# Sums of the output-weight quarters: from GpSimd subtractions to ScalarE negations and adding transfers

## The chip, the core and the metric

The kernel runs on one core of a Trainium2 chip. The metric is the device time of one execution in microseconds (us); the time before is the median of three executions, 1373.9 us (1372.88 to 1374.18). The profile is of one further execution, whose span is 1369.5 us. The engines are called PE (TensorE), DVE (VectorE), ACT (ScalarE), POOL (GpSimd) and SP (SyncE, which only issues transfers here).

## What is computed

An attention block with a threshold, followed by a feed-forward block. Cut to what matters:

```python
# q, k, v: (8, 8, 576, 64) float32; tau: a scalar
scores = q @ k.T / sqrt(64)
thresh = max(scores, -1) - tau
scores = where(scores >= thresh, scores, -1e9)
attn = softmax(scores)                      # exp, divided by the sum + 1e-9
x = (attn @ v), heads side by side          # (4608, 512)
# w_in: (512, 2048), w_out: (2048, 512)
h = x @ w_in
g = h / (1 + exp(-1.702 * h))
out = g @ w_out                             # (4608, 512) float32
```

The feed-forward weights arrive as float64 and are converted to float32 on the chip.

## The kernel before

**Attention** goes by pairs of heads, 32 pairs `n` in all, four to a batch. For each pair PE makes transposed scores in five tiles (`scores`, `scores_two`, `tail_scores`, lines 462 to 487), ACT copies them out of PSUM (`keep`, `keep_two`, L498 and L512), DVE finds maxima (`in_groups` L526, then `over_tiles` L532 and L537, then `over_groups` L546 and L547, small operations on 64 or 32 partitions), DVE subtracts the threshold (`sub`, L598), ACT masks (L609) and exponentiates (L613), PE multiplies by the values (`values`, L627), and DVE sums, inverts and places the product into `xT` (L698). POOL copies a small key tail into `kd` for the fifth score tile (`prep_kd`, L452).

**Feed-forward** goes by blocks of 256 rows. The first two blocks are done plainly by `first_blocks`: `mm1_0` (L753), tanh, gelu, `mm2` (L735), and `half` (L742), an ACT copy with a scale out of PSUM. From block `PLAIN` = 2 on, `feed_forward` computes the hidden layer with `mm1` (L713), ACT's `tanh` (L722) and DVE's `gelu` (L725), which frees one of two PSUM banks for the next `mm1`. The second product (`second`, `product`, L900) is Strassen-Winograd's: both the gelu output and `w_out` are cut into four quarters, and seven products of quarters or sums of quarters replace eight. The last four blocks use the same scheme for the first product too (`two_blocks`, `product1`, L818).

The gelu output's sums are made for each block on POOL (`s_sums`, L866 to L868, and `s_last`, L879). The sums of the quarters of `w_out` are made once and stay. With `qb[f][m]` the quarters of `w_out` (each 128 partitions by 8 rows by 256 columns):

```python
t1, t2, t4 = tw
t3 = qb[0][1]
T_SUMS = [(t1, t3, qb[0][0]), (t2, qb[1][1], t1), (t4, qb[1][0], t2), (t3, qb[1][1], t3)]   # out = a - b
```

`t3` is made in place of a quarter of `w_out`, and `t4` lies where `first_blocks` keeps its gelu output; both may be written only when the first two blocks are done. `t1` and `t2` need only the converted `w_out`. In the kernel before, the four sums are eight POOL operations of half a quarter each, queued after the first `s_sums` of block 2. The products that read them are P6 (`t2`), P7 (`t3`), P4 (`t4`) and P5 (`t1`).

**The order of work.** All engines' instructions are put in order when the program is built, by a planner in the kernel: `task(engine, cost, rank, function, ..., after, take, give, lag)` names a cost in us, a rank, the tasks it waits for, the buffers it takes and gives, and the time from its end until others may use its result. `run_in_order` plays this forward: a free engine takes the ready task of lowest rank whose buffers are free. Feed-forward products on PE have rank `LAST`, so they fill what attention leaves; tanh, gelu and sums have `FIRST`. On the chip each engine works its list in that order and waits at each instruction for its semaphores. So a change of a task's engine, cost or lag moves other instructions too. Weight conversion is also among these tasks: `load_w` (POOL transfers, L399 and L400), `cv_power` on ACT (L418), and `cv_end` on DVE (L436), which writes a piece of `w_in` or `w_out`.

Of the kernel before, what the change touches and what calls it, by code (L numbers as in the profile page):

```python
# [14 lines left out]
AF = mybir.ActivationFunctionType  # L15
ALU = mybir.AluOpType
# [14 lines left out]
def kernel(  # L31
# [34 lines left out]
    nc = tc.nc  # L66
# [11 lines left out]
    HF = d_ff // P // 2  # L78
# [132 lines left out]
    def task(engine, cost, rank, f, *a, after=(), take=(), give=(), lag=None):  # L211
        if lag is None:
            lag = LAG[engine]
        if 0 <= rank < LAST:
            rank += CV.get(f.__name__, 0.0) + (EARLY if a[0] < 2 * NPAIR else LATER).get(f.__name__, 0.0)
        tasks.append((engine, cost, rank, f, a, [x for x in after if x is not None],
                      take, give, lag))
        return len(tasks) - 1

    FIRST, LAST = -9.0, 1000.0  # L220
# [101 lines left out]
    def own(n, *pools):  # L322
        return tuple(x + "_apart" for x in pools) if n in APART else pools
# [33 lines left out]
    n_in = len(pieces)  # L357
# [7 lines left out]
    def stage(i):  # L365

        if i < n_in:
            return i % (STAGES + 2) if i % (STAGES + 2) < STAGES else None
        i -= n_in
        return STAGES - 1 if i % 3 == 0 and i < NFC - PER_STAGE else None  # L370
# [376 lines left out]
    PLAIN = 2  # L747
# [107 lines left out]

    T_SUMS = [(t1, t3, qb[0][0]), (t2, qb[1][1], t1), (t4, qb[1][0], t2), (t3, qb[1][1], t3)]

    def t_sum(x, k):
        o, a, b = (y[:, ts(k, 4), :] for y in T_SUMS[x])
        nc.gpsimd.tensor_tensor(out=o, in0=a, in1=b, op=ALU.subtract)  # L860

    def s_sums(k):

# [18 lines left out]
    P1, P2, P6, P7, P4, P5, P3 = range(7)  # L882
# [56 lines left out]
    for h in range(2):  # L939
        nc.gpsimd.memset(ones_t[ts(h, D), h, :], 1.0)  # L940
    nc.gpsimd.dma_start(
        out=tau_b, in_=bass.AP(tensor=tau.tensor, offset=tau.offset, ap=[[0, P], [1, 1]])
# [28 lines left out]
    WHOLE = 6  # L971

    FFU = 1.727

    W_IN, W_OUT = (3.11, 1.53), (2.49, 2.62)
    ready_w, w_loads = [], []
    for i in range(len(pieces)):
# [7 lines left out]
        x = stage(i)  # L985
        place = ("w64",) if x is None else (f"stage{x}",)
        a = task("POOL", 1.1, rank, load_w, i, after=w_loads[-1:], take=place, lag=9.0)
# [3 lines left out]
        a = task("DVE", 1.1, rank, cv_frac, i, after=[e])  # L991
# [8 lines left out]
    placed, spread, ffn = {}, {}, []  # L1000
    last_mm2, t_ready = {}, []

    def first_blocks():
        xs = list(placed.values())[-NPAIR:]
        for j in range(NFC):
            for i in range(PLAIN):
                x = j * P // WC
                ffn.append(task(
                    "PE", FFU, LAST, mm1_0, j, i,
                    after=ffn[-1:] + xs + ready_w[x * NDC : (x + 1) * NDC],  # L1010
# [4 lines left out]
        for i in range(PLAIN * BLK // P):  # L1015
            for p in range(NFC // 2):
                after = ffn[-1:] + [gelus[2 * p], gelus[2 * p + 1]]
                after += ready_w[n_in + 2 * p : n_in + 2 * p + 2]
                ffn.append(task(
                    "PE", FFU, LAST, mm2, i, p, after=after, take=("psM",) if p == 0 else (),  # L1020
                ))
# [2 lines left out]
            task("SP", 0.6, FIRST, store_0, i, after=[a], give=("osb",), lag=2.2)  # L1024


    def feed_forward(blk):
        b = -(-(blk + 1) * BLK // S) - 1
        xs = [placed[n] for n in range(NPAIR * (b + 1))]
        sums = []  # L1030
        for j in range(HF):
            for f in range(2):
                after = ffn[-1:] + xs[-NPAIR:]
                last = j == HF - 1 and f == 1
                ffn.append(task(
                    "PE", FFU, LAST, mm1, blk, j, f, after=after,
                    take=("psM",) if f == 0 else (), give=("xT",) if last else (),
                ))
            a = task("ACT", 0.48, FIRST, tanh, j, after=ffn[-1:], take=("io",))
            gelus[j] = task(  # L1040
                "DVE", 0.59, FIRST, gelu, j, after=[a, last_mm2.get(j // 4)],
                give=("psM", "io"),
            )
            if j % 2:
                sums.append(task("POOL", 2.3, FIRST, s_sums, j // 2, after=[gelus[j - 1], gelus[j]]))
            if j == 1 and blk == PLAIN:
                for y in range(8):
                    after = t_ready[-1:] + sums[-1:] + ready_w[n_in:]
                    t_ready.append(task("POOL", 2.4, FIRST, t_sum, *divmod(y, 2), after=after))
        second(blk, 0, {j: [gelus[j]] for j in range(HF)}, sums)  # L1050

    T_OF = {P6: 4, P7: 8, P4: 6, P5: 2}

    def second(blk, w, ready, sums):
        reads = [None] * 7
# [3 lines left out]
        for x, p in order:  # L1059
            js = ((0, 4), (4, 8), (4, 7), (7, 8))[p]  # L1060
            after = ffn[-1:]
            if x in T_OF:
                after += t_ready[: T_OF[x]]
            if x in (P1, P2, P4):
# [3 lines left out]
            else:  # L1068
# [3 lines left out]
            ffn.append(task(  # L1072
                "PE", FFU / 4 * (js[1] - js[0]), LAST, product, blk, x, js, w, after=after,
                take=("psA" if w else "psM",) if x in (P1, P2) and p == 0 else (),
# [19 lines left out]
    def two_blocks(blk):  # L1094
# [18 lines left out]
        for j in range(HF):  # L1113
            reads = [None] * 7
            for x in range(7):
# [6 lines left out]
                if x == P3 or first:  # L1122
                    after += xs
                bank = (BANK_OF[(7 * j + x) % 5],)
                ffn.append(task(
                    "PE", FFU / 2, LAST, product1, blk, j, x, after=after, take=bank,
                    give=("xT", "xT") if x == P3 and j == HF - 1 else (),
# [33 lines left out]
    for n in range(NP):  # L1161
        gate = per_pair * (n - LEAD)
        after = ffn[gate : gate + 1] if gate >= 0 else []
# [7 lines left out]
        lag = (4.6, 3.0)[n] if n < 2 else 10.0 if n < 2 * NPAIR else 3.0  # L1171
# [18 lines left out]
        for t in range(NKT + 1):  # L1190
            tail = t == NKT
            copies = []
            if n >= WHOLE and not tail:
                if t % 2 == 0:
                    a = task(
                        "PE", 1.94, r, scores_two, n, t, after=[pq, pk] + after,
                        take=("psA",) * 3 + ("s_m",) * 2,
                    )
                    after = [a]
                b = task("ACT", 0.6, r, keep_two, n, t, 0, after=[a], give=("psA",))  # L1200
# [5 lines left out]
            elif tail:  # L1206
                a = task(
                    "PE", 0.97 * slow, r, tail_scores, n, after=[pq, pk, pd] + after,
                    take=("psA", "s_t"), give=own(n, "qkT0", "qkT1") + ("kd",),
                )  # L1210
                after = [a]
                copies = [task("ACT", 0.55, r, keep, n, t, 0, after=[a], give=("psA",))]
            else:
                for c in range(2):

                    a = task(
                        "PE", 0.49 * slow, r, scores, n, t, c, after=[pq, pk] + after,
                        take=("psA",) + (own(n, "s_m") if c == 0 else ()),
                    )
                    after = [a]  # L1220
                    copies.append(task("ACT", 0.55, r, keep, n, t, c, after=[a], give=("psA",)))
            mx.append(task("DVE", 0.66 if tail else 1.27, r, in_groups, n, t, ALU.max, after=copies))
        a = task("DVE", 0.8, r, over_tiles, n, ALU.max, after=mx)
        a = task("DVE", 0.86, r, over_groups, n, ALU.max, after=[a])
        if n in BY_DMA:
            a = task("DVE", 0.5, r, lower_rows, n, after=[a, tau_done], take=("row",))
            a = task("SP", 0.35, r, row_out, n, after=[a], lag=3.3)
            m = task(
                "SP", 1.5, r, row_in, n, after=[a], take=own(n, "mb") + ("mbt",), give=("row",),
                lag=5.2,  # L1230
            )
        else:
            a = task("DVE", 0.68, r, lower, n, after=[a, tau_done])
# [3 lines left out]
        for t in range(NKT + 1):  # L1237
            tail = t == NKT
            a = task(
                "DVE", (0.67 if n in BY_DMA else 1.55) if tail else 1.35, r, sub, n, t, after=subs[-1:],  # L1240
                give=own(n, "mb") + (("mbt",) if n in BY_DMA else ()) if tail else (),
            )
            subs.append(a)
            a = task("ACT", 0.59 if tail else 1.09, r, mask, n, t, after=[a])
# [3 lines left out]
        if n < NPAIR:  # L1248
# [12 lines left out]
            a = task("DVE", 1.07, r, one_row, n, after=[den], give=("psM", "psM"))  # L1261
        else:
            pv = task("PE", 4.84, r, values, n, every, after=ws + [lv], take=("psA",), give=("v_m", v_tail))
        if NPAIR <= n < BY_PE:
            a = task("PE", 4.84, r, sums_by_pe, n, every, False, after=ws + [pv], take=("psA",), give=back)
            a = task("DVE", 1.07, r, one_row, n, after=[a], give=("psA",))
        elif n >= BY_PE:
# [4 lines left out]
            a = task("DVE", 0.8, r, over_tiles, n, ALU.add, after=su + [pv], give=back)  # L1272
            a = task("DVE", 0.86, r, over_groups, n, ALU.add, after=[a])
            a = task("DVE", 0.75, r, one_group, n, after=[a])
        a = task("DVE", 1.05, r, spread_sums, n, after=[a], take=("rc",))
        b, hp = divmod(n, NPAIR)
# [6 lines left out]
        while hp == NPAIR - 1 and (next_blk + 1) * BLK <= (b + 1) * S:  # L1283
            if next_blk >= TAIL:
                if (next_blk - TAIL) % 2:
                    two_blocks(next_blk - 1)
            elif next_blk >= PLAIN:
                feed_forward(next_blk)
            elif next_blk == PLAIN - 1:
                first_blocks()  # L1290
            next_blk += 1
# [31 lines left out]
```

## Time and profile before

| | before |
|---|---|
| time, median of three | 1373.9 us |
| span of the profiled execution | 1369.5 us |
| `t_sum` on POOL (L860) | 8 operations of 128x1024 float32, 2343 to 2375 ns, from 290.7 to 309.2 us |
| ACT, all work | 638.0 us (47% of the span) |
| DMA | 78.70 MB in all, mean 57 GB/s |

How to read it: an engine's busy time counts instructions that run, also while they are held up inside. "Idle before" names the wait that ended last before an instruction. PE's busy time contains matmuls at whatever clock was granted, so PE can be busy and slow. The waits with the largest sums in the page are on engines with much idle time (POOL for gelu outputs, ACT for matmuls) and say nothing on the time by themselves.

### The profile page before, as it was taken

What the parts mean: (1) busy time and instruction counts of PE and PEld (TensorE: products, weight loads), DVE (VectorE), ACT (ScalarE), POOL (GpSimd) and SP (SyncE); (2) the same over time, 40 slices, a digit from 0 to 9 for tenths busy, and PEclk for the clock granted to TensorE, in tenths of its full rate; (3) what the DMA queues carried; (4) which work ended last, traced back from release to release, by engine and by line L of the source; (5) the groups of instructions that cost most, each with busy time, mean ns of one, the idle gap of its engine ahead of it and who ended that gap; (6) DMA issues with size and microseconds to landing.
All of it is one profiled execution on the core that took longest, in us unless ns stands there. A gap on an engine that the chain in (4) does not pass through costs nothing.

```text
span 1369.5 us, 18133 instructions
## 1 busy us (share of the span) xinstructions
PE 1315.9 (96%) x6792; PEld 1010.6 (74%) x6792; DVE 1111.1 (81%) x1906; ACT 638.0 (47%) x822; POOL 279.9 (20%) x362
## 2 busy tenths in 40 slices
PE   5769999988999999999999999999999999999999
PEld 3436764466777877787777777787778778888887
DVE  7899999899999889818999889929999698562642
ACT  4875565455455455415555455424655453110210
POOL 1202210053121211311120312021222204420120
PEclk9998999998999999999999999999999999999999
DMA  8775774111210111101112111201211000000000
GB/s 166 258 200 195 252 242 107 39 26 24 57 26 15 42 22 39 30 21 18 42 33 47 24 34 26 47 5 43 43 27 43 9 16 1 16 1 16 16 0 31
DMA packets 205379, 78.70 MB, mean 57 GB/s; under 512 B 192747, under 2 KB 192747, under 8 KB 205291
## 3 DMA queue, kind: packets, MB, share of 16 engines
q1 hardware_dynamic: 195723, 43.71, 15.0%
q0 software_dynamic: 7200, 33.55, 7.0%
q8 instruction: 53, 0.87, 0.3%
q10 hardware_dynamic: 2368, 0.30, 0.2%
q14 instruction: 35, 0.29, 0.1%
HBM read 68.05 MB, written 9.47 MB: 57 GB/s over the span
## 4 chain that ended last, share of the span: by engine, by line
PE 64%; DVE 23%; ACT 8%; issue 3%; DMA 1%; SPq 1%; DVEq 0%; ACTq 0%
PE ops L900 20%; PE hps L713 13%; PE pv L627 9%; PE ps L487 5%; DVE part L526 5%; PE ps L818 4%; DVE arena L598 4%; PE ps L900 4%; PE ops L735 3%; ACT arena L613 3%; ACT arena L609 3%; PE ops L818 3%; DVE arena L725 2%; PE ps L472 2%; DVE arena L572 1%
## 5 line engine op out<-in xcount | busy, mean ns | idle before, releaser
L713 PE MATMUL hps<-xT,w_in 128*128 128x256 f32 x1536 | 343.2, 382 | 10.9 <-DVE arena L725 10.9
L713 PEld LDWEIGHTS hps<-xT,w_in 128*128 128x128 f32 x1536 | 290.8, 191 | 61.4 <-DVE arena L725 14.3
L526 DVE TRANSPOSE_TENSOR_REDUCE part<-arena 128x36 f32<-128x1152 f32 x236 | 310.6, 1349 | 25.9 <-ACT arena L498 24.2
L900 PE MATMUL ops<-w_out,arena 128*128 128x256 f32 x896 | 206.4, 382 | 2.9 <-DVE arena L725 2.9
L613 ACT ACTIVATE arena<-arena,shift,scl 128x1152 f32<-128x1152 f32 (+1 forms) x160 | 200.0, 1250 | 4.5
L900 PEld LDWEIGHTS ops<-w_out,arena 128*128 128x128 f32 x896 | 168.1, 190 | 36.5 <-issue 8.3
L609 ACT ACTIVATE arena<-arena 128x1152 f32<-128x1152 f32 (+1 forms) x160 | 169.0, 1056 | 53.5 <-DVE arena L598 53.4
L598 DVE TENSOR_TENSOR arena<-arena 128x1152 f32<-128x1152 f32 x128 | 175.5, 1417 | 0.6
L498 ACT COPY arena<-ps 128x640 f32<-128x640 f32 x208 | 122.4, 643 | 105.0 <-PE ps L487 104.7
L722 ACT ACTIVATE th<-hps 128x512 f32<-128x512 f32 x112 | 66.3, 592 | 191.2 <-PE hps L713 175.1
L866 POOL TENSOR_TENSOR arena<-arena 128x256 f32<-128x256 f32 x56 | 51.9, 927 | 501.9 <-DVE arena L725 392.5
L900 PE MATMUL ops<-arena 128*128 128x256 f32 x672 | 152.7, 381 | 1.8 <-DVE osb L922 1.8
L900 PEld LDWEIGHTS ops<-arena 128*128 128x128 f32 x672 | 126.7, 190 | 24.0 <-issue 3.1
L627 PE MATMUL pv<-arena 128*64 128x288 f32 x960 | 124.8, 411 | 0.6 <-ACT arena L498 0.6
L487 PE MATMUL ps<-arena 64*128 64x320 f32 (+1 forms) x832 | 115.0, 416 | 0.0
L512 ACT COPY arena<-ps 128x576 f32<-128x576 f32 x80 | 49.0, 643 | 134.8 <-PE ps L472 114.7
L627 PEld LDWEIGHTS pv<-arena 128*64 128x64 f32 x960 | 66.9, 137 | 53.8 <-ACT arena L498 5.9
L725 DVE SCALAR_TENSOR_TENSOR arena<-th,hps 128x512 f32<-128x512 f32 x96 | 64.3, 670 | 48.6 <-ACT th L722 47.7
L487 PEld LDWEIGHTS ps<-arena 64*128 64x128 f32 x832 | 76.1, 186 | 32.1 <-issue 16.8
L922 DVE SCALAR_TENSOR_TENSOR osb<-ops,osb 128x256 f32<-128x256 f32 x98 | 39.0, 409 | 64.0 <-PE ops L900 59.5
L452 POOL COPY kd<-arena 64x64 f32<-64x64 f32 x64 | 15.6, 244 | 332.0 <-DVE arena L447 298.9
L447 DVE STREAM_TRANSPOSE arena<-arena 128x576 f32<-128x576 f32 x64 | 46.3, 754 | 16.3 <-PE ps L472 7.9
(125 smaller groups left out, 1510.6 us busy)
## 6 DMA issues: line engine op xcount, KB each, us to landing
arena<-in_q_dram SPq DMA_DIRECT2D x128, 72.0 KB, 2.4
out_dram<-osb SPq DMA_DIRECT2D x36, 256.0 KB, 2.0
arena<-in_k_dram SPq DMA_DIRECT2D x124, 72.0 KB, 2.3
arena<-in_v_dram SPq DMA_DIRECT2D x64, 128.0 KB, 2.4
w_out<-in_moe_w_in_dram POOLq DMA_DIRECT2D x12, 512.0 KB, 7.0
arena<-in_moe_w_out_dram POOLq DMA_DIRECT2D x12, 512.0 KB, 5.7
w_out<-in_moe_w_in_dram POOLq DMA_DIRECT2D x12, 511.6 KB, 8.2
arena<-in_moe_w_out_dram POOLq DMA_DIRECT2D x12, 511.6 KB, 6.4
```

What stands on the lines that cost most here:

```text
L487: nc.tensor.matmul(o, lhsT=mats[n, 1][ts(h, D), ts(t + u, P)], rhs=mats[n, 0][ts(h, D), qs], start=True, stop=True,)
L498: nc.scalar.copy(out=o, in_=pss.pop((n, t, c)))
L526: nc.vector.tensor_reduce(out=o, in_=i, axis=AXL.X, op=op, apply_transpose=True)
L598: nc.vector.tensor_tensor(out=s, in0=s, in1=mb, op=ALU.subtract)
L609: nc.scalar.activation(out=s, in_=s, func=AF.Prelu, alpha=STEEP)
L613: nc.scalar.activation(out=s, in_=s, func=AF.Exp, scale=scl, bias=shift)
L627: nc.tensor.matmul(o[c][ts(h, D), 0:SH], lhsT=lhsT, rhs=rhs, start=(t == 0), stop=(t == NKT),)
L713: nc.tensor.matmul(hidden[j][:, ts(f, BLK)], lhsT=w_in[:, c, ds((f * HF + j) * P, P)], rhs=xTs[blk][:, c, :], start=(c == 0), stop=(c == N ...
L722: nc.scalar.activation(out=ths[j], in_=hidden[j], func=AF.Tanh, scale=GELU_SCALE / 2)
L725: nc.vector.scalar_tensor_tensor(out=g[:, :, j, :], in0=two(ths.pop(j)), scalar=1.0, in1=two(hidden.pop(j)), op0=ALU.add, op1=ALU.mult,)
L818: nc.tensor.matmul(places[j, x], lhsT=left[:, c, ts(j, P)], rhs=right[:, c, :], start=(c == 0), stop=(c == 1),)
L900: nc.tensor.matmul(banks[blk][k][:, ts(o, HM)], lhsT=left[:, j, :], rhs=right[:, j, :], start=(j == 0), stop=(j == HF - 1),)
```

## The change

Each subtraction `out = a - b` becomes two steps: ACT writes `out = -b` (`t_minus`, two halves, an activation Copy with scale -1), and then a transfer issued by POOL adds `a` to it on its way into the SBUF (`t_plus`, `accum_op=add`, one transfer of 128 partitions by 2048 float32, 1 MB). This takes the sums off POOL's arithmetic, and makes `t1` and `t2` as soon as `w_out` is converted rather than in block 2. The tasks are now queued in `first_blocks`; the sums of `t4` and `t3` wait there for the last product of the first two blocks. The planner is told 1.0 us for each ACT step, 1.0 us on POOL for each transfer and 9.0 us until it has landed.

```diff
-    def t_sum(x, k):
-        o, a, b = (y[:, ts(k, 4), :] for y in T_SUMS[x])
-        nc.gpsimd.tensor_tensor(out=o, in0=a, in1=b, op=ALU.subtract)
+    def t_minus(x, k):
+        o, _, b = (y[:, ts(k, HF // 2), :] for y in T_SUMS[x])
+        nc.scalar.activation(out=o, in_=b, func=AF.Copy, scale=-1.0)
+
+    def t_plus(x):
+        o, a, _ = T_SUMS[x]
+        nc.gpsimd.dma_start(out=o, in_=a, accum_op=ALU.add)
...
+    T_RANK = FIRST
...
     def first_blocks():
...
+        for x in range(4):
+            after = t_ready[-1:] + (ffn[-1:] if x > 1 else []) + ready_w[n_in:]
+            for k in range(2):
+                after = [task("ACT", 1.0, T_RANK, t_minus, x, k, after=after)]
+            t_ready.append(task("POOL", 1.0, T_RANK, t_plus, x, after=after, lag=9.0))
...
     def feed_forward(blk):
...
-            if j == 1 and blk == PLAIN:
-                for y in range(8):
-                    after = t_ready[-1:] + sums[-1:] + ready_w[n_in:]
-                    t_ready.append(task("POOL", 2.4, FIRST, t_sum, *divmod(y, 2), after=after))
...
-    T_OF = {P6: 4, P7: 8, P4: 6, P5: 2}
+    T_OF = {P6: 2, P7: 4, P4: 3, P5: 1}
```

Below, "pair 0" to "pair 3" of the negations, and "transfer 0" to "transfer 3", are those of `T_SUMS[0]` to `T_SUMS[3]`, that is of `t1`, `t2`, `t4` and `t3`. `HF // 2` is 4, so a negation covers 128x1024 elements, as an operation of `t_sum` does.

## The prediction

> **What bounds the kernel now.** I read the page's busy row first, then busy time by windows, then the timelines of four engines where TensorE (PE) has a hole.
>
> ```profile
> PE 1315.9 (96%) x6792; PEld 1010.6 (74%) x6792; DVE 1111.1 (81%) x1906; ACT 638.0 (47%) x822; POOL 279.9 (20%) x362
> ...
> 303.50:312.50 9.00, 0.44 (x1) 0.44 (x2) 8.79 (x12) 0.36 (x1) 6.09 (x4) 0.61 0.06 11
> 312.50:316.00 3.50, 3.50 (x10) 2.34 (x11) 3.38 (x11) 0.00 (x0) 1.72 (x3) 0.55 0.87 141
> 316.00:342.00 26.00, 25.37 (x144) 18.94 (x143) 25.39 (x37) 18.09 (x23) 7.80 (x8) 1.00 0.03 7
> 342.00:442.00 100.00, 98.40 (x532) 75.84 (x531) 94.50 (x158) 53.46 (x67) 16.20 (x22) 1.00 0.17 33
> 642.00:1142.00 500.00, 496.39 (x2644) 389.85 (x2643) 440.38 (x746) 257.94 (x325) 97.30 (x119) 1.00 0.14 30
> ```
>
> Columns: stretch and length; busy us (and instructions) of PE, its weight loads, VectorE (DVE), ScalarE (ACT), GpSimd (POOL); granted clock; DMA share; GB/s. PE is 96% busy, and over 98% from 342 us on, so the kernel is PE-bound once it is full. A saving counts only where it fills PE idle time or lifts PE's clock. One place stands out after the fill: in 303.5 to 312.5 PE does 0.44 us of work in 9, and in the next 3.5 us its clock is 0.55.
>
> ```profile
> 297.89 5.34 PE L713 MATMUL hps<-xT,w_in 128*128 128x256 f32 x24
> 312.06 3.75 PE L713 MATMUL hps<-xT,w_in 128*128 128x256 f32 x8 [8.83 <-DVE arena L725]
> ...
> 290.65 4.70 POOL L860 TENSOR_TENSOR arena<-w_out 128x1024 f32<-128x1024 f32 x2
> 295.31 9.28 POOL L860 TENSOR_TENSOR arena<-w_out,arena 128x1024 f32<-128x1024 f32 x4
> 304.54 4.64 POOL L860 TENSOR_TENSOR w_out<-w_out 128x1024 f32<-128x1024 f32 x2
> ...
> 296.24 0.36 DVE L532 TENSOR_REDUCE red<-part 128x36 f32<-128x144 f32 x1
> 296.63 3.38 DVE L537 TENSOR_TENSOR red<-red,part_t 64x18 f32<-64x18 f32 x2
> 300.05 2.28 DVE L546 COPY fold<-red 64x36 f32<-64x36 f32 x1
> 302.36 2.27 DVE L547 TENSOR_TENSOR red<-red,fold 64x36 f32<-64x36 f32 x1
> 304.67 2.25 DVE L546 COPY fold<-red 32x36 f32<-32x36 f32 x1
> 306.95 2.27 DVE L547 TENSOR_TENSOR red<-red,fold 32x36 f32<-32x36 f32 x1
> ...
> 311.36 0.65 DVE L725 SCALAR_TENSOR_TENSOR arena<-th,hps 128x512 f32<-128x512 f32 x1
> ```
>
> Columns: start, duration, engine, line, operation, count, and in brackets the idle time before it with its releaser. The eight quarter sums (L860) hold POOL from 290.65 to 309.2. In that time DVE's tiny reductions take 2.3 us each. The same instructions take 0.18 or 0.19 us at 217 us (0.36 for the two at L537). Behind them in DVE's queue stands the gelu of L725, which frees a PSUM bank; PE waits 8.83 us for it and restarts at a low clock. No wait for a quarter sum itself appears: the harm is to DVE.
>
> **What the Trainium skill says.** "SBUF — State Buffer", section "Who interferes with whom": VectorE and GpSimd share a port pair by an exclusive lock; a two-input VectorE operation, or a copy in a 2-port mode, fully blocks behind a GpSimd instruction that reads SBUF, while `tensor_reduce` does not contend. The trace agrees in detail: the reduce of 296.24 keeps 0.36 us, and the six two-input operations and copies after it lose 3.02+2.10+2.08+2.08+2.08 = 11.4 us. The same section says that DMA uses ports of its own and ScalarE waits for nobody, so neither replacement should bring the lock back. "Collectives: The Full Stack", section "The bandwidth ceiling", says that an adding transfer is slow not for its addition but because it reads two sources. No run here shows that yet.
>
> **The change, part by part.** *Removed:* eight POOL operations, 4.70+9.28+4.64 = 18.6 us, with 11.4 us of blocked DVE time. PE regains the idle 8.83 us; the slow restart, 3.75 us for 8 matmuls against 1.9 us for 8 at 277.3 us, so 1.9; and 0.63 us of idle at 332.8 in the same block, also a late gelu. Sum 11.3 us. Would PE have idled anyway? Unblocked, the DVE chain from 296.24 reaches L725 near 300.4 us, where its tanh is ready, and PE needs it at 303.2. So no.
>
> *Added on ACT:* eight negating copies of 128x1024. ACT's mask, L609, takes 1.16 us for 1152 columns and 0.67 for 576: 0.85 ns a column, so 1.05 us each, 8.4 us in all. ACT has 53% idle, so only their places count. The instruction order of the changed kernel shows four pairs:
> - Pair 0, right after the last converted piece of w_out, at 213.4 us of before. It stands between score copies. Their PSUM banks are needed again only after six more matmul steps (the order puts 5.4 us of them before the next scores), and ACT then idles 7.4 us before the next mask at 227.7. Cost near nothing.
> - Pair 1, in that same gap, but it must wait for transfer 0 (below).
> - Pair 2, when the first two blocks are done (about 276 us), ahead of four score copies and the nine masks and exponentials of a pair. These end near 295 us instead of 290; but the new order puts 12 more steps of matmuls (5.3 us) before the PV product that needs them, which so moves from 291.8 to about 297. Hidden.
> - Pair 3, between two tanh of the first Strassen block. A tanh late by up to 2.1 us, with two PSUM banks at 3.6 us of matmuls each, can stall PE some 0.5 us. I book 0.8 us for both pairs.
>
> *Added transfers:* four of 128x2048 f32 (1 MB), issued by POOL (0.54 us each for the weight loads). The trace has no adding transfer. The nearest rows are the weight loads, of which two of 512 KB go out together:
>
> ```profile
> arena<-in_moe_w_out_dram POOLq DMA_DIRECT2D x12, 512.0 KB, 5.7
> arena<-in_moe_w_out_dram POOLq DMA_DIRECT2D x12, 511.6 KB, 6.4
> ...
> 219.69 0.64 ACT L512 COPY arena<-ps 128x576 f32<-128x576 f32 x1 [1.75 <-PE ps L472]
> 227.70 1.17 ACT L609 ACTIVATE arena<-arena 128x1152 f32<-128x1152 f32 x1 [7.38 <-DVE arena L598]
> ...
> 240.12 4.10 PE L627 MATMUL pv<-arena 128*64 128x288 f32 x32
> ```
>
> A megabyte thus lands in 6.4+0.5 = 7 us there, and that is my lower end. From "DMA: Bandwidth & Descriptors", section "Anatomy of one DMA", 2.0 us plus bytes over 436 GB/s gives 4.4 us for a plain copy; reading twice gives an estimate of 2.0+4.8 = 6.8. Here the pieces are 1 KB, and query and key loads run beside it, so I take 8 us; the upper end, if small pieces and the addition cost double or more, is 20 to 25. For transfer 0 this decides. It leaves at about 216 us and lands at 224; pair 1 then ends at 226.3, before the mask at 227.7. Each us above 9.5 delays all of ACT's queue behind pair 1, that is the masks and exponentials at 227.7 to 239.5, for which PE's product at 240.12 waits with 0.6 us to spare. So about (landing time minus 10) would go to PE.
>
> The other three are far from their readers. Transfer 1 leaves near 226.5; behind it in POOL's queue stands a key copy that isn't ready before 237. Transfer 2 leaves at 278 with row sums behind it that are ready at 288 to 290. Transfer 3 leaves near 291, and its first reader comes after the second PV product, about 330. Even 25 us fits.
>
> *Moved:* the order on PE differs only from about 215 to 440 us of before; from there to the end it is the same list, and changes between score, value and feed-forward work number the same (180). So the gain carries to the end, since PE is over 98% busy there. In 342 to 442 us DVE is 94.5% busy, so a little could leak; but DVE itself gets 11.4 us back.
>
> **Sum.** 11.3 - 0.8 = 10.5 us; 1373.9 - 10.5 = 1363.4 us.
>
> **Rivals.**
> - *Slow adding transfer (slower).* At 25 us from issue, pair 1 ends at 243.3, the masks are 15.6 us late, PE loses 15: 1363.4 + 15 = 1378 us. At 20 us it loses 10, and 1373 is no change. For it: no row shows such a transfer, and the gap is filled to within 1.5 us. Against: the loads of the same size, and the skill's account of two reads.
> - *Half given back.* With DVE near 95% and ACT's queue lengthened, tanh and mask come late in the new order, and new holes of 4 to 6 us open between 280 and 440 us: 1368 us. For it: two banks leave a tanh little room. Against: DVE regains more than PE needs, and before shows only 1.6 us of holes in 342 to 442.
> - *Nothing changes.* The hole is only moved, since other DVE work limits this stretch: 1374 us. Against: the hole falls exactly into the POOL operations, and DVE's lost time exceeds it.
>
> **How the numbers follow.** Full gain, 1361 to 1365.5: 0.72. Half given back, 1365.5 to 1370.5: 0.14. No change, within 2.7 us, by a 20 us transfer or a moved hole: 0.05. Slower: 0.09. The range 1360 to 1369.5 takes the first case and most of the second. Faster is 0.86.
>
> **What would show it.** In the new profile: no POOL operation of 2.35 us; the small DVE reductions at 0.2 us throughout and DVE's busy sum near 1100; ACT's near 646; PE's wait of 8.83 us for L725 gone and its clock at 1.0 in 303 to 316 us; landing of the adding transfers below 10 us. I am wrong if ACT's first mask after pair 1 waits for a transfer, if PE waits for an exponential near 240 us, or if the holes reappear behind tanh between 280 and 330 us.

## The result, and the profile after

The changed kernel takes 1359.4 us, median of four runs (1358.8 to 1359.8); the kernel before, timed beside it, 1373.4 us (1372.3 to 1374.2). The ratio is 0.9898, 95% interval 0.9881 to 0.9915: 14.0 us or 1.0% faster. A later repetition gave 1359.4 against 1373.3 us. The forecast was 1363.4 us with a range down to 1360.0, so the direction and the cause of the hole came as written, but the gain was 3.5 us larger than forecast, and the time lies 0.6 us past the edge of the range.

The page of the changed kernel, its busy row and the granted clock in 40 slices:

```profile
PE 1313.2 (97%) x6792; PEld 1010.0 (74%) x6792; DVE 1098.1 (81%) x1906; ACT 645.0 (48%) x830; POOL 268.2 (20%) x358
...
PEclk9888999999999999999999999999999999999999
```

The profiled execution of the kernel before took 1371.3 us, less than its median, so the two profiles differ by 12.5 us (spans of 1369.5 and 1357.0 us) and not by 14.0. In them PE does the same 6792 matmuls in 2.7 us less, DVE lost 13.0 us of busy time for the same 1906 instructions, ACT gained 7.0 us. POOL fell by only 11.7 us although 18.6 us of subtractions are gone, mostly because its instructions that issue the four adding transfers are long themselves (below).

Busy time by windows, kernel before, the two stretches around the old quarter sums (columns as in the prediction):

```profile
300.00:345.00 45.00, 35.54 (x181) 26.85 (x181) 43.61 (x65) 19.15 (x25) 19.60 (x18) 0.89 0.13 24
345.00:446.00 101.00, 99.40 (x537) 76.71 (x536) 94.87 (x160) 53.86 (x66) 16.18 (x22) 1.00 0.16 33
```

The same view of the kernel after:

```profile
300.00:345.00 45.00, 45.00 (x249) 34.58 (x246) 41.48 (x86) 20.58 (x27) 9.73 (x12) 1.00 0.23 41
345.00:446.00 101.00, 100.93 (x547) 78.80 (x545) 96.84 (x162) 57.26 (x71) 14.83 (x20) 1.00 0.18 38
```

PE was idle for 9.46 + 1.60 = 11.06 us of these 146 us and is now idle for 0.07, with the clock at 1.0 throughout. In the first 45 us it starts 249 matmuls instead of 181. Note the second row: the 1.6 us of small holes there also went. The prediction named these holes, and did not count them as a gain.

The timeline of DVE after, at the chain of small reductions that had been held up (start, duration, engine, line, operation):

```profile
299.99 0.39 DVE L532 TENSOR_REDUCE red<-part 128x36 f32<-128x144 f32 x1
300.41 0.36 DVE L537 TENSOR_TENSOR red<-red,part_t 64x18 f32<-64x18 f32 x2
300.80 0.18 DVE L546 COPY fold<-red 64x36 f32<-64x36 f32 x1
301.02 0.19 DVE L547 TENSOR_TENSOR red<-red,fold 64x36 f32<-64x36 f32 x1
```

L546 and L547 take 0.18 and 0.19 us in place of 2.28 and 2.27, and the pair at L537 0.36 in place of 3.38. Nothing of POOL's arithmetic lies beside them any more.

What replaces the sums, from ACT's timeline of the kernel after, where transfer 0 has to land before pair 1 can start:

```profile
213.85 2.03 ACT L860 ACTIVATE arena<-w_out 128x1024 f32<-128x1024 f32 x2
...
225.51 2.00 ACT L860 ACTIVATE arena<-arena 128x1024 f32<-128x1024 f32 x2 [1.23 <-DMA arena<-w_out]
229.95 1.16 ACT L609 ACTIVATE arena<-arena 128x1152 f32<-128x1152 f32 x1 [2.44 <-DVE arena L598]
```

Pair 0 ends at 215.9; pair 1 waits 1.23 us for the transfer; and after pair 1 ACT still waits 2.44 us, for DVE, before the first mask. That 2.44 us is the slack of the whole chain: pair 1 may be so much later before anything else is.

The group of POOL's adding transfers (L864) after: count, issue time in ns (minimum, median, maximum), and the time to landing:

```profile
L864 POOL DMA_DIRECT2D arena<-w_out x3: 1529/1557/1606, 216.2 to 278.5; - x3
...
DMA to landing us min/median/max: 9.2/9.3/9.6
```

They land in 9.2 to 9.6 us, and each holds POOL for 1.5 to 1.6 us at issue, four times 1.56 = 6.2 us: that is most of the difference between 18.6 us and the 11.7 by which POOL's sum fell.

### The profile page after: what moved, and what is told of

Same layout as the page of the kernel before. It is cut to its first block, busy times and chain, and to the rows that moved or that the text cites. A ratio compares the mean times of both kernels' runs of the same rounds, so it can differ in the third digit from the quotient of the medians.

```text
span 1357.0 us, 18154 instructions
## 1 busy us (share of the span) xinstructions
PE 1313.2 (97%) x6792; PEld 1010.0 (74%) x6792; DVE 1098.1 (81%) x1906; ACT 645.0 (48%) x830; POOL 268.2 (20%) x358
## 3 DMA queue, kind: packets, MB, share of 16 engines
q0 software_dynamic: 11360, 37.74, 9.3%
## 4 chain that ended last, share of the span: by engine, by line
PE 67%; DVE 21%; ACT 8%; issue 3%; DMA 1%; SPq 0%; DVEq 0%; ACTq 0%
PE ops L904 21%; PE hps L713 14%; PE pv L627 10%; PE ps L487 5%; PE ps L818 4%; DVE part L526 4%; DVE arena L598 4%; PE ps L904 4%; PE ops L735 3%; ACT arena L613 3%; PE ops L818 3%; ACT arena L609 3%; PE ps L472 2%; DVE arena L725 1%; DVE arena L572 1%
## 5 line engine op out<-in xcount | busy, mean ns | idle before, releaser
L598 DVE TENSOR_TENSOR arena<-arena 128x1152 f32<-128x1152 f32 x128 | 176.7, 1426 | 2.4 <-DMA arena<-row 1.8
L883 POOL TENSOR_TENSOR arena<-arena 128x512 f32<-128x512 f32 x28 | 39.6, 1417 | 102.2 <-PE ops L904 102.2
```

The costliest lines, as they stand in the source:

```text
L598: nc.vector.tensor_tensor(out=s, in0=s, in1=mb, op=ALU.subtract)
```

## The experiments

The question was twofold: is the gain really the lock between POOL's subtractions and DVE, and where do the 3.5 us beyond the forecast come from? All times below are medians; the kernel before was re-timed beside each group at 1372.9, 1373.8 and 1373.3 us.

**e1: the old order without the sums.** The products that read `t2`, `t4` and `t1` read plain quarters of `w_out` instead; the planner still plans the eight POOL tasks.

```diff
     def t_sum(x, k):
-        o, a, b = (y[:, ts(k, 4), :] for y in T_SUMS[x])
-        nc.gpsimd.tensor_tensor(out=o, in0=a, in1=b, op=ALU.subtract)
+        return
```

> The kernel before with its own order, only the eight GpSimd subtractions left out: the sums of the w_out quarters are not made, and the products that used t2, t4 and t1 read quarters of w_out instead. Lock theory (the time lost before is DVE blocked behind GpSimd's two-input subtractions): the hole of 8.8 us and the slow restart vanish, 1360 to 1362 us, DVE busy near 1100 us. Order theory (the gain of the change comes from the new order of the feed-forward work): the order is that of before, so less than 3 us is gained, 1371 to 1373.

Measured: 1362.3 us (1361.0 to 1363.4), ratio 0.9922 (0.9909 to 0.9936). Taking away the subtractions and nothing else is worth 10.6 us, with an interval of 8.8 to 12.5. PE's timeline of e1 between 300 and 446 us, its waits:

```profile
323.33 2.43 PE L899 MATMUL ops<-w_out,arena 128*128 128x256 f32 x10 [0.84 <-DVE arena L725]
...
388.18 2.00 PE L713 MATMUL hps<-xT,w_in 128*128 128x256 f32 x8 [0.66 <-DVE arena L725]
...
418.60 3.72 PE L899 MATMUL ops<-w_out,arena 128*128 128x256 f32 x16 [0.93 <-DVE osb L921]
```

The 8.83 us hole is gone, so it was the subtractions' doing. Three small holes are left, 2.43 us together, of which the first is the 0.63 us hole that the prediction had put down to the sums. It stays without them.

**e2: the new order without the sums.** In the changed kernel `t_minus` and `t_plus` emit nothing; the same products read plain quarters.

> The changed kernel with its own order, but neither negations nor adding transfers: the sums are not made, and the products that used t2, t4 and t1 read quarters of w_out instead. If what the change adds is wholly hidden: 1359.4 us within 1 us. If the negations and transfers cost PE the 0.8 us that the prediction booked, or more: 1357 to 1358.6.

Measured: 1358.7 us (1358.3 to 1358.9), ratio 0.9896 (0.9882 to 0.9909). e1 and e2 do the same work, neither makes any sum; they differ in the order of instructions alone. Every run of e2 is below every run of e1, by 3.6 us between the medians. So some 3.6 us of the gain are the new order's. The profiled spans say nearly the same, 1360.6 and 1357.1 us. Busy time from 300 to 446 us, first e1, then e2:

```profile
300.00:446.00 146.00, 143.49 (x770) 111.35 (x769) 137.86 (x235) 75.50 (x94) 26.54 (x35) 1.00 0.19 37
300.00:446.00 146.00, 145.93 (x795) 113.63 (x792) 138.29 (x247) 77.71 (x97) 24.51 (x32) 1.00 0.19 38
```

PE is idle for 2.51 us in e1's order, and for 0.07 us in the new one. Later repetitions of the two orders put the difference between 2.2 and 3.6 us (e10 and e12, below).

**e3: the subtractions back on POOL, at their new place.** In the order of the changed kernel, `t_minus` emits nothing and `t_plus` makes two POOL subtractions in place of the transfer.

```diff
     def t_plus(x):
-        nc.gpsimd.dma_start(out=o, in_=a, accum_op=ALU.add)
+        for k in range(2):
+            o, a, b = (y[:, ts(k, HF // 2), :] for y in T_SUMS[x])
+            nc.gpsimd.tensor_tensor(out=o, in0=a, in1=b, op=ALU.subtract)
```

> The changed kernel's order, but no negations, and in place of each adding transfer two GpSimd subtractions as before, so the same 18.7 us of GpSimd work at four earlier places. Lock theory: DVE is blocked at 216, 228, 278 and 291 us, by 8 to 12 us in all, and part of it reaches PE at the value product near 240 us: 1364 to 1370 us. Order theory: 1359 to 1361 us, since order and place are those of the changed kernel.

Measured: 1368.9 us (1368.2 to 1369.5), ratio 0.9970 (0.9959 to 0.9981), 9.5 us slower than the changed kernel with the same PE order. DVE's timeline of e3, at the first two subtractions (213.5 to 218.4 us), shows whom they hold up there:

```profile
213.65 2.60 DVE L424 TENSOR_SCALAR arena<-arena 128x512 int32<-128x512 int32 x1
216.28 2.71 DVE L428 SCALAR_TENSOR_TENSOR arena<-arena 128x512 int32<-128x512 int32 x1
```

These steps of weight conversion take 0.42 and 0.69 us elsewhere. PE's timeline of e3 has the consequence, a wait for the converted piece of `w_out`:

```profile
219.84 6.19 PE L735 MATMUL ops<-w_out,arena 128*128 128x512 f32 x10 [4.43 <-DVE w_out L436]
```

The lock goes wherever the subtractions go. Both operations, a two-input one and a `TENSOR_SCALAR`, are among those that the Trainium skill, "SBUF — State Buffer", section "Who interferes with whom", names as able to contend with GpSimd; here each lost about 2 us.

**e4: negations and adding transfers at the old place.** They are queued in `feed_forward` where `t_sum` was.

```diff
             if j == 1 and blk == PLAIN:
-                for y in range(8):
-                    after = t_ready[-1:] + sums[-1:] + ready_w[n_in:]
-                    t_ready.append(task("POOL", 2.4, FIRST, t_sum, *divmod(y, 2), after=after))
+                for x in range(4):
+                    after = t_ready[-1:] + sums[-1:] + ready_w[n_in:]
+                    for k in range(2):
+                        after = [task("ACT", 1.0, FIRST, t_minus, x, k, after=after)]
+                    t_ready.append(task("POOL", 1.0, FIRST, t_plus, x, after=after, lag=9.0))
```

> Negations on ScalarE and adding transfers as in the change, but queued where the subtractions stood before, after the first row sums of block 2. Lock theory: the engines matter and not the place, 1359 to 1363 us, no blocked DVE operations near 300 us. Order theory: most of the gain is gone, 1368 us or more.

Measured: 1367.6 us (1366.5 to 1368.9), ratio 0.9960 (0.9948 to 0.9973). A miss for the number expected of the lock, and yet the lock is gone: there is no hole at 303 us, and L546 is short in e4's timeline of DVE:

```profile
297.85 0.18 DVE L546 COPY fold<-red 64x36 f32<-64x36 f32 x1
```

What is left over is put down to order here, by argument and not by a run: no run holds e4's order without the sums. For it: PE's list differs from that of before from 335 us of before to nearly the end, none of PE's holes in e4 names a negation or an adding transfer as its releaser, and the longest one after 300 us (2.2 us, at 1159 us) comes long after the sums are made. PE is idle for 9.8 us between 345 and 1340 us against 5.5 in the changed kernel. Busy time by windows of e4, the second stretch:

```profile
345.00:446.00 101.00, 97.92 (x526) 76.37 (x524) 93.93 (x161) 52.98 (x64) 18.16 (x20) 1.00 0.18 37
```

3.1 us idle here, where the changed kernel has 0.07. The same negations and transfers, at another place and in another order, thus take 8.2 us more than in the order of the change.

**e5: small pieces.** Each adding transfer is cut into eight of 32 columns; all orders stay as they are.

```diff
-        nc.gpsimd.dma_start(out=o, in_=a, accum_op=ALU.add)
+        for c in range(8):
+            nc.gpsimd.dma_start(
+                out=o[:, :, ts(c, HM // 8)], in_=a[:, :, ts(c, HM // 8)], accum_op=ALU.add
+            )
```

> The changed kernel, each adding transfer cut into eight of 32 columns, so that transfer 0 lands later (eight issues of 1.5 us, then some 8 us: near 20 us after its first issue instead of 9.3). If the slack is what the traces show (pair 1 may start up to 2.4 us later before ScalarE's masks are late), pair 1 starts near 237 us, the masks come some 8 us late and PE idles 6 to 9 us near 241 us: 1365 to 1369 us. If transfers are hidden whatever they take: 1359.4 us.

Measured: 1367.4 us (1366.3 to 1369.5), ratio 0.9958 (0.9946 to 0.9971), 8.0 us above the changed kernel. ACT's timeline of e5:

```profile
236.57 2.00 ACT L860 ACTIVATE arena<-arena 128x1024 f32<-128x1024 f32 x2 [12.40 <-DMA arena<-w_out]
238.48 1.15 ACT L609 ACTIVATE arena<-arena 128x1152 f32<-128x1152 f32 x1
```

And its list of PE's waits (sum, times, longest):

```profile
PE pv L627 <- ACT arena L613: 4.5, 4, 1.6
```

Pair 1 starts 11.1 us later than in the changed kernel. The slack of 2.44 us is used up, the remaining 8.6 us push every mask and exponential behind it, and PE waits for those. No wait of PE for POOL's key copy is in that list, although the sixteen issues of transfers 0 and 1 hold POOL twice for 12.5 us. This is the rival "slow adding transfer" made real: the danger that the prediction described exists, and the change avoids it by landing in 9.3 us.

**e6: the eight subtractions on DVE**, at the place of the negations, planned at 1.15 us each.

```diff
-        nc.gpsimd.tensor_tensor(out=o, in0=a, in1=b, op=ALU.subtract)
+        nc.vector.tensor_tensor(out=o, in0=a, in1=b, op=ALU.subtract)
```

> The eight subtractions on DVE instead, 1.15 us each by the 128x1152 row, at the early place; other orders shift with it. If what counts is DVE time alone, 9.2 us more of it where DVE is 90% busy gives back 2 to 9 us: 1361 to 1368 us, but better than GpSimd's subtractions, which cost DVE 11.4 us. If only the port pair counts: 1359 to 1361 us.

Measured: 1367.6 us (1366.2 to 1368.4), ratio 0.9953 (0.9938 to 0.9968). An operation took 1.2 us on DVE, but the order also differs to the end of the kernel, and PE is idle for 7.1 us between 446 and 1142 us against 4.5 after. DVE's load and the order can't be told apart here; the run decides nothing.

**e7: negations on POOL**, the adding transfers kept.

```diff
-        nc.scalar.activation(out=o, in_=b, func=AF.Copy, scale=-1.0)
+        nc.gpsimd.tensor_single_scalar(out=o, in_=b, scalar=-1.0, op=ALU.mult)
```

> Adding transfers as in the change, but the negations on GpSimd instead of ScalarE: one-input operations that read the SBUF. The order on PE is that of before. If any GpSimd operation that reads the SBUF blocks DVE's two-input operations, DVE operations beside the negations take 1 us or more longer and the time is 1363 to 1367 us. If only GpSimd operations with two inputs block: the 1362.3 us of the kernel before without sums, within 1 us.

Measured: 1370.3 us (1367.2 to 1371.3), ratio 0.9973 (0.9962 to 0.9984), slower than either number expected. PE's order is that of before, so e1's 1362.3 us is what to set it against: 8.0 us slower. The group of POOL's negations of e7 (count, ns, place), then a line of DVE's timeline of e7:

```profile
L860 POOL TENSOR_SCALAR arena<-arena x4: 2759/2772/3800, 228.8 to 279.7; 128x1024 f32<-128x1024 f32 x4
```

```profile
282.45 8.24 DVE L598 TENSOR_TENSOR arena<-arena 128x1152 f32<-128x1152 f32 x4
```

Four of L598 take 5.16 us after. A negation with a single input on POOL holds up DVE as the subtraction did, and takes longer than it (2.76 against 2.35 us). The issue of an adding transfer doesn't: in the changed kernel the issue of transfer 2, at 278.5 us, lies beside three of L598, which take 3.90 us, 1.30 each. So what frees DVE in the change is the move to ACT and to the transfers; a single-input form on POOL would not have done.

**e8: plain copies in place of the adding transfers.** `accum_op` is left out; all orders stay.

> The changed kernel with plain copies in place of the adding transfers (so t1, t2, t4 and t3 hold a and not a - b), to time the addition by itself. If the second read is what an adding transfer costs, the copy lands about 2.4 us earlier, near 7 us. If issue and piece size set it, the copy also lands near 9 us. The time stays at 1359.4 us within 1 us either way.

Measured, one run: 1359.5 us, as the changed kernel. The landing of L864 in e8:

```profile
DMA to landing us min/median/max: 5.1/6.2/6.8
```

The adding transfer takes 9.3 - 6.2 = 3.1 us more a megabyte, of which some 0.66 is in the issue (0.88 to 0.91 us instead of 1.53 to 1.61). But e8 changed more than the addition. The rows of POOL's queue (packets, MB, share) in before, after and e8:

```profile
q0 software_dynamic: 7200, 33.55, 7.0%
q0 software_dynamic: 11360, 37.74, 9.3%
q0 software_dynamic: 8288, 37.74, 8.0%
```

An adding transfer went out as (11360 - 7200) / 4 = 1040 packets, the plain copy of the same megabyte as (8288 - 7200) / 4 = 272. So e8 doesn't show whether the second read or the smaller packets make the difference. At the kernel's end nothing is seen of it in this one execution, as it lies within the slack.

**e9 and e10: the changed kernel again, and the new order without sums again**, side by side.

> The changed kernel itself, once more, beside the next two on the same chip: 1359.4 us within 0.7 us.

> The changed kernel's order without negations and adding transfers (products read quarters of w_out instead), beside the changed kernel. If the additions cost PE the booked 0.8 us: 0.5 to 1.1 us below the changed kernel. If they are wholly hidden: less than 0.4 us below it.

Measured: e9 1359.4 us (1358.8 to 1359.9), e10 1359.4 us (1358.0 to 1360.8). The negations and transfers of the change cost nothing that these times can show; with e10 spread over 2.8 us, and e2 0.7 us below the changed kernel, they can't exclude some tenths either. The traces show no such cost: PE is idle from 213 to 446 us for 0.34 and 0.47 us with the negations (the changed kernel and e9), and for 0.45 and 0.30 without (e2 and e10).

**e11: pairs 0, 1 and 2 negated twice.** The order of instructions stays; ACT does 6.3 us more.

```diff
-        nc.scalar.activation(out=o, in_=b, func=AF.Copy, scale=-1.0)
+        for _ in range(1 if x == 3 else 2):
+            nc.scalar.activation(out=o, in_=b, func=AF.Copy, scale=-1.0)
```

> The changed kernel with each negation of pairs 0, 1 and 2 done twice, 6.3 us more of ScalarE work at the same places. If ScalarE's queue has slack there, the time rises by less than 0.5 us; if the negations already cost PE time, by 2 us or more. Pair 1 ends 2.1 us later, inside the 2.4 us that were left before the mask; pair 2 delays masks and exponentials that end about 2 us before their product.

Measured: 1367.0 us (1364.7 to 1367.4), ratio 0.9952 (0.9940 to 0.9965): 7.6 us slower, against my own expectation. ACT's timeline of e11:

```profile
213.44 4.20 ACT L861 ACTIVATE arena<-w_out 128x1024 f32<-128x1024 f32 x4
...
230.65 4.18 ACT L861 ACTIVATE arena<-arena 128x1024 f32<-128x1024 f32 x4 [6.79 <-DVE arena L598]
234.74 1.15 ACT L609 ACTIVATE arena<-arena 128x1152 f32<-128x1152 f32 x1
```

The landing of its transfer 0, issued at 217.94 us:

```profile
DMA to landing us min/median/max: 12.6/12.6/12.6
```

217.94 + 12.6 is 230.5, so pair 1 waited for the transfer, although DVE is named as the releaser: a wait is put down to the event that came last, and here both came about then. The sum against the changed kernel: issue 1.75 us later, landing 3.4 us slower, doubled pair 1 2.2 us longer, less the slack of 2.44, makes 4.9; the first mask is 4.8 us late (234.74 against 229.95), and PE is busy for 81.5 us between 213 and 300 where it was for 86.7. That is 5.2 of the 5.9 us between the two profiles; the profiled execution is the fastest of e11, and the rest of the 7.6 is not traced. The slower landing was not foreseen: the later transfer ran beside the loads of threshold rows, which took 8.3 us for 576 KB instead of 4.0. So ACT at 48% of the span has some 2 us to spare at this place, not the half.

**e12: the old order's tasks dropped from the plan.** As e1, but the planner does not keep POOL's 19.2 us for the sums either.

```diff
-            if j == 1 and blk == PLAIN:
-                for y in range(8):
-                    after = t_ready[-1:] + sums[-1:] + ready_w[n_in:]
-                    t_ready.append(task("POOL", 2.4, FIRST, t_sum, *divmod(y, 2), after=after))
```

> As e1, but the planner's eight POOL tasks for the sums are left out too, so that the plan no longer keeps 19.2 us of POOL for them; products P4, P5 and P6 read plain quarters in place of the sums. This gives a third order without any sum, put in order by the planner from 270 us on. Theory A: the 3.6 us between e1 and e2 come from the POOL time that the old plan kept, which pushed the hidden layer's and the products' steps later; then 1358 to 1360 us, as e2, and no PE wait over 0.3 us between 300 and 446 us. Theory B: they come from where this one order happens to put its steps, and a third order gives a third value: then anything of 1361 us or more, with holes behind gelu as in e1 or a tail as in e4 (1367).

Measured: 1361.6 us (1361.4 to 1363.4), ratio 0.9924 (0.9910 to 0.9937), as e1. PE's waits in e12 between 300 and 446 us, from its timeline:

```profile
322.85 2.43 PE L899 MATMUL ops<-w_out,arena 128*128 128x256 f32 x10 [0.85 <-DVE arena L725]
...
387.69 2.00 PE L713 MATMUL hps<-xT,w_in 128*128 128x256 f32 x8 [0.67 <-DVE arena L725]
...
418.13 3.72 PE L899 MATMUL ops<-w_out,arena 128*128 128x256 f32 x16 [0.94 <-DVE osb L921]
```

The same three holes as in e1. The third order that was expected did not come about: by the source lines in the traces, PE, DVE and ACT run the same sequence in e12 as in e1, and two POOL instructions alone moved. So the POOL time that the plan kept did not shape PE's list, theory A falls, and e12 is in effect e1 again. The new tasks at their early place in `first_blocks` shift the list from 215 us on, and in that order the holes don't occur. e7 says which: it has the same tasks, at the same place, with the same rank and the same 9 us until landing, but the negations are POOL's, and there PE's order is that of before, with the three holes (0.85, 0.67 and 0.93 us). It is the ACT steps in the plan that move PE's list.

## Where the prediction was right, and the step that failed

*The bound and the mechanism* were right. The lock between POOL's subtractions and DVE's small operations made the hole: e1 removes it by removing the subtractions alone, and e3 brings a hole back at the new place by putting them back.

*Removed, 11.3 us.* Measured 10.6 (8.8 to 12.5) from before to e1, and 11.7 to e12, so the sum holds within its interval. Of its terms, the 8.83 us wait went. The 0.63 us at 332.8 did not belong to the sums: e1 and e12 still have that hole, at 0.84 and 0.85 us.

*Added on ACT, 0.8 us booked.* Not seen: e9 and e10 agree to 0.1 us, and PE's idle time beside them is the same to 0.2 us with and without. ACT's negations take 1.05 us each as worked out (2.03 and 2.00 for two), ACT's sum is 645 us where 646 follow from the forecast's 8.4, and the value product behind pair 2 starts at 297.57 us where about 297 was given. The comparison with an idle share alone would have been wrong, as e11 shows; the gap at each place was the right thing to read.

*Transfers.* The estimate of 8 us was short; they land in 9.2 to 9.6. The reserve held all the same: pair 1 ended at 227.5, just inside the 227.7 of the forecast. That it had 2.44 us left was luck, since the forecast did not see that DVE would release the first mask only at 229.95. The account in the Trainium skill, "Collectives: The Full Stack", section "The bandwidth ceiling", is of the adding step of a collective, which it calls slow by its second read. The estimate of 6.8 - 4.4 = 2.4 us for that read stands beside 3.1 measured, but e8 changed the packets too, so no run here shows that cause.

*Moved, taken as nothing.* This is the step that failed. The prediction read the new order on PE for one question, whether the gain carries to the end, and treated the order itself only as a risk ("a little could leak"). It never asked what the new order does with the small holes that before already shows in 342 to 442 us. They went. e1 to e2 measures the order by itself: 3.6 us, where the sum has nothing. With the spans of the profile: idle between 300 and 446 us is 2.51 us in e1 and 0.07 in e2, which makes 2.4, and the same matmuls are busy for 1314.4 and 1313.0 us, which makes 1.4; together 3.8, against 3.5 between the spans. The 2.4 us are the three holes, of which the forecast had booked the first, the 0.63 us at 332.8, under what is removed. The 1.4 us can't be put down to the order: e10 is the same program as e2, and its profile has 2.5 us more of PE time. The busy rows of e2 and e10:

```profile
PE 1313.0 (97%) x6792; PEld 1012.4 (75%) x6792; DVE 1097.8 (81%) x1906; ACT 638.0 (47%) x822; POOL 261.4 (19%) x354
PE 1315.5 (97%) x6792; PEld 1011.7 (74%) x6792; DVE 1097.5 (81%) x1906; ACT 638.3 (47%) x822; POOL 261.3 (19%) x354
```

So 2.4 us of the order's gain are traced to holes, and the rest of it is within what executions of one program differ by.

So the 14.0 us are, to within noise, 10.6 of lock, 3.6 of order, and nothing for what was added; the forecast had 11.3, 0 and -0.8. The repetitions e12 and e10 would divide them as 11.7 and 2.2, so the split is known to about 1 us, and the order's part is above nothing either way. The range missed by 0.6 us since it was built from the lock's terms upward from 1360, with no term for an order that helps. Of the rivals, the slow transfer is real (in e5 pair 1 starts 20.5 us after the first issue and the kernel loses 8.0 us, where the forecast gave 10 for a landing at 20), "half given back" is what e4 measured, at 1367.6 us, and not the change, and "nothing changes" is refuted by e1.

## What to carry to other kernels

When an engine's tiny operations take ten times their usual time (here 2.3 us against 0.2), look at what runs beside them, not at what they wait for: no list of waits showed the lock, the durations did. Where a planner orders the instructions, a change is two changes: run the old and the new order with the disputed work left out of both, and book the difference (2.2 to 3.6 us here) as the order's. Compare the lists too: a run that is meant to have another order may have the same one, as e12 had. Slack belongs to a place and not to an engine: an engine at 48% of the span had about 2 us to give before one chain, and 6.3 us more of its work at three places cost 7.6, in part by way of a transfer that went out later and landed 3.4 us slower.

## What was not expected of the hardware

A GpSimd multiplication by a constant, one input of 128x1024 float32, took 2.76 to 3.80 us, more than a subtraction of two such inputs at 2.34 to 2.38. The Trainium skill, "GPSIMD Engine Reference", section "Engine selection", calls one-input operations roughly line-rate; ACT's negation of the same size took 1.05 us, and even a two-input subtraction on DVE 1.2 us (e6), so this case doesn't agree. An adding transfer of 1 MB within the SBUF lands 3.1 us after a plain copy would (9.3 against 6.2), and its issue holds POOL for 1.56 us instead of 0.9. Eight issues of 128 KB each held POOL for 12.5 us (e5), again 1.57 each: the issue's time did not shrink with the size. The number of packets didn't either. Less the 7200 of before, POOL's queue has 33280 packets in e5's 32 issues, 1040 for each, as many as for the whole megabyte. The plain copy, with 272, took 0.9 us to issue. In these three cases the time of the issue went with the packets, not with the bytes.
